# Transposing LayerNorm row tiles by a DMA transfer instead of by TensorE

## The chip, the core and the metric

The kernel runs on one NeuronCore of a Trainium2 chip. The metric is the device time of one execution in microseconds, from start to end as the runtime measures it. Lower is better.

## What is computed

Four residual layers over one sequence of 2048 rows and 576 features, in bf16: attention, gated MLP, attention, gated MLP. Each layer first normalises its input row by row (no learned scale). The attention is local and dilated: 32 heads of 18 features, and each position looks at itself and the seven positions 2, 4, ..., 14 rows before it. The gated MLP has a spatial product, in which a 2048x2048 matrix mixes the rows.

```python
def _layernorm(x, axis=-1, eps=1e-05):
    m = jnp.mean(x, axis=axis, keepdims=True)
    v = jnp.var(x, axis=axis, keepdims=True)
    return (x - m) / jnp.sqrt(v + eps)

def _A_ref(x, wqkv, wo):            # W, dil = 8, 2
    ...
    idx = pos[:, None] - off[None, :]
    ...
    logits = jnp.einsum('bhsd,bhswd->bhsw', q, kg) * scale
    attn = _softmax(jnp.where(mask, logits, -1000000000.0), axis=-1)
    o = jnp.einsum('bhsw,bhswd->bhsd', attn, vg)
    return o.transpose(0, 2, 1, 3).reshape(B, S, D) @ wo

def _B_ref(x, w_in, w_sp, b_sp, w_out):   # F = 4608, Fh = 2304
    z = _gelu(jnp.einsum('bsd,df->bsf', x, w_in))
    z1 = z[..., :Fh].copy()
    z2 = _layernorm(z[..., Fh:], axis=-1)
    g = jnp.einsum('ts,bsf->btf', w_sp, z2) + b_sp[None, :, None]
    return jnp.einsum('bsf,fd->bsd', z1 * g, w_out)

x = x + _A_ref(_layernorm(x, axis=-1), A_wqkv, A_wo)
x = x + _B_ref(_layernorm(x, axis=-1), B_w_in, B_w_sp, B_b_sp, B_w_out)
x = x + _A_ref(_layernorm(x, axis=-1), A_wqkv, A_wo)
x = x + _B_ref(_layernorm(x, axis=-1), B_w_in, B_w_sp, B_b_sp, B_w_out)
```

## The kernel before

The kernel has five phases: F (0 to about 252 us of the profiled execution), S (to 572), F (to 888), S (to 1206) and E (to the end).

**Phase F** makes an attention layer and the second half of the following MLP's input product. It is a pipeline of small steps, each on one engine. In order:

- *Row tiles for the attention.* There are 16 tiles of 128 rows. In the first F phase `LNX_steps` loads a tile of the input (x_in) and normalises it. In the second, `p3_steps` first makes the tile: it multiplies zu, the result of the S phase before, by the output weights (p_ps), adds the residual (x, L323), stores the sum to DRAM (xres) and normalises it.
- *`ln_steps`* is the normalisation, shared by all: `.s` takes statistics on VectorE (ln_st), `.p` makes the scale and offset on GpSimd, `.n` writes the normalised rows xn (bf16, 640 columns: 512 and the last 64 twice) on ScalarE, `.t` transposes xn by five TensorE transposes against the identity into PSUM (ln_tp), and `.e` copies that to xnD on VectorE or ScalarE, whichever the planner finds free.
- *xnD* is the transposed activation: 128 partitions, five chunks of features, and one column for each row of the sequence, with PADL = 14 columns of zeros ahead of row 0. All later products read it.
- *Queries and keys* (`QK_steps`): nine groups of 228 new columns, five products each (qk_ps), copied to stg, written to a DRAM buffer (qk_bounce) and read back in another layout (QK).
- *Values* (`V_steps`) and *attention* (`ATT_steps`): 18 tiles of 114 rows. L_ps is the logits, P the exponentials, O_ps the weighted values, o_t the quotient; w_ps is the output product, xw the new residual, stored to xres. Each such tile is then normalised by `ln_steps` too (114 rows, the last 110) and overwrites its columns of xnD.
- *`Z2_steps`* multiplies xnD by the second half of the input weights (z_ps), with GELU and normalisation into zu.

**Phase S** makes the first half of the input product from xnD and w1 (z_ps, L739), the spatial product (g_ps, L746, 32 matmuls for each of 72 tiles) and the gating. The spatial matrix w_sp comes transposed into W: four transfers of 512x2048 for each phase, issued from SP at L727. **Phase E** is the last output product.

The order of the work within a phase F is not written by hand. `Flow` takes the steps with their engine, an estimated duration, a key (smaller goes first), what they come after, and the buffers that they take (`caps`: three PSUM tiles H, two PT for transposes, three xn, three xw, three x in the second F phase). `order` plays them through and issues each engine's instructions in the order found. Each engine then works its queue in that order, and waits on hardware semaphores only. A step's successor may start `lag` after its end in the planner's time; 0.12 us for a compute step, and 2.2 to 6 us for a transfer (LX for a load, LW for a bounce write, LR for the read back). A buffer is free again, for the planner, at the end of its last user. The keys of the row tiles are `2 * g - KX` for the group g that needs them, those of QK group g `2 * g - KQ`, and those of attention tile t are about t; one key unit is one attention tile. All transfers within a phase F, save a few weights, go through SP's queue (`self.dma`, L164).

The matmuls of the values read xnD with a column step of 2. `wrote_xn` and `read_xn_strided` tell the framework which of these and which writes of xnD share columns.

Of the kernel before, what the change touches and what calls it, by code (L numbers as in the profile page):

```python
# [16 lines left out]
P = 128  # L17
HP = 64
S = 2048
# [7 lines left out]
QT = P - HALO  # L27
QH = QT // 2
PADL = HALO
NT = 18  # L30
NS = S // P
NG = NT // 2
GW = 2 * QT + HALO
GH = GW // 2
XW = QT * (NT - 1) + P
NB = 9
NZ = 10
NM = D // P
WA = 6
EPS = 1e-5  # L40
LX, LW, LR, KQ, KX = 5, 5.0, 6.0, 6.5, 8.0
SCALE = DH ** -0.5


# [104 lines left out]
class K:  # L149
# [16 lines left out]
    def setup(self):  # L166
        nc, tc, ctx = self.nc, self.tc, self.ctx
        c = self.base = ctx.enter_context(tc.tile_pool(name="base", bufs=1))
        self.dram = ctx.enter_context(tc.tile_pool(name="dram", bufs=1, space=DRAM))
        self.xres = [self.dram.tile([S, D], f32, name=f"xres{i}") for i in range(3)]  # L170
        self.ps = ctx.enter_context(tc.tile_pool(name="ps", bufs=1, space=PSUM))
        self.ident = c.tile([P, P], bf16, name="ident")
        self.maskT = c.tile([P, QH], bf16, name="maskT")
        self.mask0 = c.tile([P, QH], bf16, name="mask0")
        self.xnD = c.tile([P, NM + 1, XW], bf16, name="xnD")
        self.zu = c.tile([P, NZ, 2 * S], bf16, name="zu")
        self.wA = c.tile([P, WA * 2, D], bf16, name="wA")
        self.neg_half = c.tile([P, 1], f32, name="neg_half")
        make_identity(nc, self.ident[:])
        nc.vector.memset(self.neg_half[:], -0.5)  # L180
        self.xn_writes, self.xn_strided = [], []
        self.wrote_xn(nc.vector.memset(self.xnD[:, :, 0:PADL], 0.0), 0, PADL)
        self.wrote_xn(nc.vector.memset(self.xnD[:, :, PADL + S:XW], 0.0), PADL + S, XW)

    def masks(self):

# [56 lines left out]
        if not rest_first:  # L243
            rest(False)

    def ln_steps(self, fl, tag, key, row0, n, x, after, uses=(), guard=()):

        nc, pool, box = self.nc, self.pool, {}

        def stats(_):  # L250
            st = box["st"] = pool.tile([P, 2 * nc.vector.BN_STATS_DIM + 4], f32, name="ln_st", bufs=6)
            m = 2 * nc.vector.BN_STATS_DIM
            v = st[:, 0:m].rearrange("p (s d) -> p s d", s=2)
            box["s"] = [st[:, m + k:m + k + 1] for k in range(4)]
            for s in range(2):
                nc.vector.bn_stats(out=v[:n, s, :], in_=x()[:n, s * 288:(s + 1) * 288])  # L256
            nc.vector.bn_aggr(out=st[:n, m:m + 2], in_=v[:n, :, :])  # L257

        def small(_):
            mean, var, rstd, nmr = box["s"]  # L260
            nc.gpsimd.tensor_scalar_add(out=rstd[:n], in0=var[:n], scalar1=EPS)  # L261
            nc.gpsimd.tensor_tensor(out=rstd[:n], in0=rstd[:n], in1=self.neg_half[:n, :], op=ALU.pow)
            nc.gpsimd.tensor_scalar(out=nmr[:n], in0=mean[:n], scalar1=rstd[:n], scalar2=-1.0,
                                    op0=ALU.mult, op1=ALU.mult)

        def norm(_):
            xn = box["xn"] = pool.tile([P, D + HP], bf16, name="xn", bufs=3)
            mean, var, rstd, nmr = box["s"]
            last = x()[:n, None, NM * P:D].to_broadcast([n, 2, HP])
            for out, in_ in ((xn[:n, 0:NM * P], x()[:n, 0:NM * P]),  # L270
                             (xn[:n, NM * P:].rearrange("p (a b) -> p a b", a=2), last)):
                nc.scalar.activation(out=out, in_=in_, func=ACT.Identity, scale=rstd[:n], bias=nmr[:n])  # L272

        def trans(_):
            tp, xn = self.PTt("ln_tp"), box["xn"]
            box["tp"] = tp
            for c in range(NM + 1):
                nc.tensor.transpose(tp[:, c, :n], xn[:n, c * P:c * P + P], self.ident[:n, :n])  # L278

        cols = slice(PADL + row0, PADL + row0 + n)  # L280

        def evac(e):
            self.wrote_xn(self.copy(e, self.xnD[:, 0:5, cols], box["tp"][:, :, :n]), cols.start, cols.stop)

        fl.step(tag + ".s", "DVE", 1.15, key, stats, after, uses, takes=[("ln_st", tag + ".st")])
        fl.step(tag + ".p", "POOL", 1.2, key, small, [tag + ".s"], [tag + ".st"])
        fl.step(tag + ".n", "ACT", 1.15, key, norm, [tag + ".p"], [tag + ".st", *uses], takes=[("xn", tag + ".xn")])
        fl.step(tag + ".t", "PE", 0.3, key, trans, [tag + ".n"], [tag + ".xn"], takes=[("PT", tag + ".tp")], mode="w")
        fl.step(tag + ".e", ("DVE", "ACT"), 0.72, key, evac, [tag + ".t", *guard], [tag + ".tp"])

# [7 lines left out]
    def p3_steps(self, fl, i, key, wout, x_prev, li, after=()):  # L298
# [43 lines left out]
        if last:  # L342
            fl.step(tag + ".o", "ACT", 0.7, key, toout, [tag + ".a"], [tag + ".x"], takes=[("ob", tag + ".ob")])
            fl.step(tag + ".w", "SP", 0.35, key, store, [tag + ".o"], [tag + ".ob"], lag=2.2)
        else:
            fl.step(tag + ".w", "SP", 0.35, key, store, [tag + ".a"], [tag + ".x"], lag=2.2)
            self.ln_steps(fl, tag, key, i * P, P, lambda: box["x"], [tag + ".a"], [tag + ".x"])

# [1 line left out]
    def phase_F(self, li):  # L352
# [52 lines left out]
        def LNX_steps(i, key):  # L405
            box, tag = {}, f"lnx{i}"

            def load(_):
                box["x"] = pool.tile([P, D], bf16, name="x_in", tag="xb", bufs=8)
                self.dma(box["x"][:], self.A_x[i * P:(i + 1) * P, :])  # L410
            fl.step(tag + ".l", "SP", 0.4, key - 3 if i > 1 else -30, load, takes=[("xb", tag + ".x")], lag=2.2 if i < 2 else LX)
            self.ln_steps(fl, tag, key, i * P, P, lambda: box["x"], [tag + ".l"], [tag + ".x"])

        def feeds(c0, n):

# [5 lines left out]
        def QK_steps(g, key):  # L421
# [5 lines left out]
            for d in range(5):  # L427
                M = 126 if d < 4 else 72

                def mm(rest_first, d=d, M=M):  # L430
                    ps = box[d] = self.Ht("qk_ps")
                    cols, at = slice(126 * d, 126 * d + M), slice(c0, c0 + GW)
                    self.mm576(lambda s: ps[:M, s, 0:GW], rest_first,
                               lambda s, c: (wqk[:, c, s, cols], self.xnD[:, c, at]),
                               lambda s, rows: (wqk_r[rows, cols], self.xnD[rows, NM, at]))

                def ev(e, d=d, M=M):
                    stg = box[d, "s"] = pool.tile([P, 2, 2, GH], bf16, name="stg", bufs=6)
                    self.copy(e, stg[:M], box[d][:M, :, 0:GW].rearrange("p q (j r) -> p q r j", r=2))

                def wr(_, d=d, M=M):
                    self.dma(box["bn"][126 * d:126 * d + M], box[d, "s"][:M])
                fl.step(f"{tag}.m{d}", "PE", 1.02, key, mm, feeds(c0, GW) + ["wqk"], takes=[("H", f"{tag}.ps{d}")], mode="wn")
                fl.step(f"{tag}.e{d}", ("DVE", "ACT"), dict(DVE=0.67, ACT=0.58), key, ev, [f"{tag}.m{d}"], [f"{tag}.ps{d}"],
                        takes=[("stg", f"{tag}.s{d}")])
                fl.step(f"{tag}.w{d}", "SP", 0.4, key, wr, [f"{tag}.e{d}", tag + ".b"], [f"{tag}.s{d}", tag + ".bn"],
                        lag=LW)
# [11 lines left out]
        def V_steps(t, key):  # L459
            box, v = {}, vb[t % 3]  # L460

            def mm(rest_first):
                ps = box["ps"] = self.Ht("v_ps")
                c0 = QT * t

                def part(first, wide):
                    for c in range(NM) if wide else (NM,):
# [130 lines left out]
        def Z2_steps(i, key, after):  # L598
# [5 lines left out]
            def mm(u):  # L604
                def f(rest_first):
                    ps = box[u] = self.Ht("z_ps")
                    at, cols = slice(PADL + i * P, PADL + i * P + P), slice(384 * u, 384 * u + 384)
                    self.mm576(lambda s: ps[:, s, 0:384], rest_first,
                               lambda s, c: (self.xnD[:, c, at], (win2a[:, c, s] if c < NM - 1 else win2b[:, s])[:, cols]),
                               lambda s, rows: (self.xnD[rows, NM, at], win2r[rows, cols]))  # L610
                return f
# [94 lines left out]
    def phase_S(self, li):  # L706
# [21 lines left out]
        for jj in range(NB):  # L728
# [6 lines left out]
            z2 = self.zu[:, jj, :].rearrange("p (i s r) -> p i s r", i=NS, s=2)  # L735
            for q in range(4):
                ps = self.Ht("z1_ps")
                at = slice(PADL + 512 * q, PADL + 512 * q + 512)
                self.mm576(lambda s: ps[:, s, :], q % 2 == 1, lambda s, c: (w1[:, NM * s + c, :], self.xnD[:, c, at]),  # L739
                           lambda s, rows: (w1[rows, 2 * NM, :], self.xnD[rows, NM, at]))  # L740
                nc.scalar.activation(out=u[:, :, 512 * q:512 * (q + 1)], in_=ps[:], func=ACT.Gelu_apprx_tanh)  # L741
# [87 lines left out]
```

## Time and profile before

| | |
|---|---|
| median of 3 runs | 1278.86 us (1276.73 to 1284.46) |
| the profiled execution's own time | 1280.8 us |
| its span, first to last instruction | 1278.8 us |
| mean granted TensorE clock | 0.989 |
| busy: TensorE, VectorE, ScalarE, GpSimd | 1239.6, 556.4, 414.1, 198.6 us |
| first F phase / second F phase | 0 to 252 us / 572 to 888 us |
| transposes of normalised tiles (L278) | 340, five for each of 68 tiles |

The page gives each engine's busy time and its share of the span. In its table of slices the span is cut into 40 equal parts, and each digit is a busy share in tenths. Windows of time give busy microseconds and, in brackets, the number of instructions of each engine, then the granted TensorE clock as a share of full speed, and the DMA engines' mean busy share and rate. PEld is TensorE's weight load, which overlaps its matmuls. SPq is SP's instruction queue, from which transfers are issued.

### The profile page before, as it was taken

To read this page: it belongs to the slowest core of one execution; us is meant where nothing else is said; L and a number is where in the kernel's file an instruction comes from. 1 tells how busy PE (TensorE), PEld (TensorE's weight loads), DVE (VectorE), ACT (ScalarE), POOL (GpSimd) and SP (SyncE) were. 2 spreads that over 40 slices of the span, in tenths; PEclk is the share of its full clock that TensorE was granted. 3 is DMA by queue.
4 is the path that set the end of the run, shared out by engine and by line. 5 is a ranking of instruction groups with operands and counts; after the bars stand their busy time and mean duration, and the time that the engine had idled before them with its cause. 6 is when DMAs were issued, how large, how long until landed. Compare 5 with 4: busy or idle time off the path is not lost.

```text
span 1278.8 us, 27787 instructions
## 1 busy us (share of the span) xinstructions
PE 1239.6 (97%) x12182; PEld 728.2 (57%) x12244; DVE 556.4 (44%) x901; ACT 414.1 (32%) x662; POOL 198.6 (16%) x494
## 2 busy tenths in 40 slices
PE   7999989999999999999999999999999999999998
PEld 6787755444444444448788876554444444444576
DVE  5777666523232323334455675663333232222311
ACT  5744687701111111001435456875100011111011
POOL 5211146700000000001112111575000000000000
PEclk9999899999999999999999998999999999999999
DMA  7655315560000000035545354185300000000232
GB/s 201 165 147 143 87 34 101 122 156 10 10 10 10 10 10 1 1 104 172 148 129 142 110 136 136 34 169 112 99 2 10 10 10 10 10 1 1 79 104 68
DMA packets 142877, 96.31 MB, mean 75 GB/s; under 512 B 92084, under 2 KB 127604, under 8 KB 142756
## 3 DMA queue, kind: packets, MB, share of 16 engines
q1 hardware_dynamic: 142068, 92.17, 28.1%
q0 software_dynamic: 688, 2.38, 0.7%
q8 instruction: 95, 1.56, 0.5%
q14 instruction: 26, 0.21, 0.1%
HBM read 51.19 MB, written 26.55 MB: 61 GB/s over the span
## 4 chain that ended last, share of the span: by engine, by line
PE 89%; DVE 4%; ACT 2%; POOL 2%; issue 1%; DMA 1%; SPq 0%; POOLq 0%; DVEq 0%; ACTq 0%
PE g_ps L746 39%; PE z_ps L241 19%; PE p_ps L316 11%; PE qk_ps L241 6%; PE z_ps L235 3%; PE O_ps L523 3%; PE v_ps L471 3%; PE w_ps L570 2%; PE ln_tp L278 1%; PE qk_ps L235 1%; ACT xn L272 1%; PE o_tp L550 1%; DVE ln_st L256 1%; DVE xw L575 1%; DMA wB<-in_B_w_in_dram 1%
## 5 line engine op out<-in xcount | busy, mean ns | idle before, releaser
L746 PE MATMUL g_ps<-W,zu 128*128 128x512 bf16 x2256 | 497.7, 379 | 2.5
L746 PEld LDWEIGHTS <-zu 128*128 128x128 bf16 x2304 | 225.4, 98 | 271.8
L751 DVE TENSOR_TENSOR g_tmp<-g_ps,bsp 128x512 f32<-128x512 f32 x144 | 99.0, 687 | 437.9 <-PE g_ps L746 437.9
L741 ACT ACTIVATE zu<-z_ps 128x1024 bf16<-128x1024 f32 x72 | 73.7, 1023 | 514.4 <-PE z_ps L235 477.1
L241 PE MATMUL z_ps<-xnD,w 128*128 128x512 bf16 x562 | 132.1, 379 | 1.2 <-issue 0.6
L316 PEld LDWEIGHTS <-zu 128*128 128x128 bf16 x1152 | 111.7, 98 | 31.2 <-DVE zu L752 2.1
L241 PE MATMUL z_ps<-wA,xnD 128*128 128x384 bf16 x576 | 109.9, 327 | 3.9 <-DVE xw L575 3.9
L316 PE MATMUL p_ps<-wA,zu 128*128 128x288 bf16 x768 | 106.0, 286 | 0.5 <-ACT v_ext L296 0.5
L241 PEld LDWEIGHTS <-xnD 128*128 128x128 bf16 x768 | 70.8, 98 | 59.8 <-issue 18.5
L752 DVE TENSOR_TENSOR zu<-g_tmp,zu 128x512 bf16<-128x512 f32 x144 | 99.7, 692 | 9.6
L241 PEld LDWEIGHTS <-w 128*128 128x128 bf16 x576 | 52.7, 97 | 75.2 <-issue 15.7
L241 PE MATMUL qk_ps<-xnD,wqk 128*126 128x242 bf16 (+1 forms) x720 | 91.3, 275 | 2.9 <-DVE o_t L532 1.3
L615 ACT ACTIVATE zu<-z_ps 128x768 bf16<-128x768 f32 x96 | 77.1, 804 | 34.5 <-PE z_ps L235 20.6
L241 PEld LDWEIGHTS <-wqk 128*126 128x126 bf16 (+1 forms) x720 | 76.6, 135 | 10.5 <-issue 7.0
L508 ACT ACTIVATE P<-L_ps 128x912 bf16<-128x912 f32 x72 | 65.0, 943 | 18.1 <-PE L_ps L501 18.0
L625 DVE CUSTOM_DVE_ANT_1 zu<-zu 128x1536 bf16<-128x1536 bf16 x32 | 56.3, 1758 | 29.9 <-ACT zu L615 29.9
L261 POOL TENSOR_SCALAR ln_st<-ln_st 114x1 f32<-114x1 f32 (+1 forms) x68 | 20.1, 296 | 306.7 <-DVE ln_st L257 245.5
L323 DVE TENSOR_TENSOR x<-p_ps,x 128x576 f32<-128x576 f32 x32 | 24.2, 758 | 89.3 <-PE p_ps L316 89.3
L295 DVE CAST stg<-qk_ps 126x484 bf16<-126x484 f32 (+1 forms) x64 | 42.2, 660 | 32.0 <-PE qk_ps L235 20.1
L570 PE MATMUL w_ps<-wo,oT 128*114 128x288 bf16 (+1 forms) x360 | 52.4, 292 | 1.6 <-ACT zu L615 1.4
L471 PE MATMUL v_ps<-wv,xnD 128*64 128x288 bf16 x576 | 46.4, 310 | 1.9 <-DVE o_t L532 1.2
L523 PE MATMUL O_ps<-v_ext,P 64*64 64x19 bf16 x2304 | 43.6, 176 | 4.5 <-issue 1.6
(79 smaller groups left out, 1114.3 us busy)
## 6 DMA issues: line engine op xcount, KB each, us to landing
QK<-qk_bounce SPq DMA_DIRECT2D x72, 136.1 KB
x<-xres SPq DMA_DIRECT2D x32, 288.0 KB
xres<-xw SPq DMA_DIRECT2D x34, 256.5 KB
qk_bounce<-stg SPq DMA_DIRECT2D x72, 119.1 KB
w<-in_B_w_in_dram SPq DMA_DIRECT2D x36, 128.0 KB
xres<-x SPq DMA_DIRECT2D x16, 288.0 KB
xw<-xres SPq DMA_DIRECT2D x17, 256.5 KB
wA<-in_B_w_in_dram SPq DMA_DIRECT2D x12, 288.0 KB
```

The lines of the kernel that those rows point to most:

```text
L241: nc.tensor.matmul(ps(s), lhsT=lhsT, rhs=rhs, start=(c == 0 and not rest_first), stop=(c == NM - 1 and rest_first))
L316: nc.tensor.matmul(ps[:, hh, 0:288], lhsT=u[:, s * S + i * P:s * S + (i + 1) * P], rhs=wout(b, s)[:, hh * 288:(hh + 1) * 288], start=(b == ...
L471: self.read_xn_strided(nc.tensor.matmul(ps[HP * par:HP * par + HP, s, 0:288], lhsT=self.xnD[rows, c, c0 + par:c0 + P:2], rhs=wv[:, c, s, : ...
L508: nc.scalar.activation(out=Psb[:, 2 * hh:2 * hh + 2, :, 0:QH], in_=box["L"][hh][:, :, 0:8 * QH].rearrange("p a (b c) -> p a b c", c=QH), f ...
L523: nc.tensor.matmul(O[rows, h // 16, (h % 16) * (DH + 1):(h % 16 + 1) * (DH + 1)], lhsT=Psb[rows, h % 4, h // 4, :], rhs=v[rows, h, :], sta ...
L570: nc.tensor.matmul(box["ps"][:n, hh, 0:288], lhsT=box["oT"][:, c, :n], rhs=wo[:, c, hh * 288:(hh + 1) * 288], start=(c == 0), stop=(c == 4))
L615: nc.scalar.activation(out=self.zu[:, 3 * u:3 * u + 3, 256 * i:256 * (i + 1)].rearrange("p j (s r) -> p s j r", s=2), in_=box[u][:, :, 0:3 ...
L625: nc.vector.tensor_tensor_reduce(out=junk(0, 6), in0=z[:, 0:6, :], in1=z[:, 0:6, :], scale=1.0 / FH, scalar=0.0, op0=ALU.mult, op1=ALU.add ...
L741: nc.scalar.activation(out=u[:, :, 512 * q:512 * (q + 1)], in_=ps[:], func=ACT.Gelu_apprx_tanh)
L746: nc.tensor.matmul(ps[:, s, :], lhsT=z2[:, i, s, :], rhs=W[q][:, i, :], start=(i == 0), stop=(i == NS - 1))
L751: nc.vector.tensor_tensor(out=tmp[:], in0=ps[:, s, :], in1=bsp[:, 512 * q:512 * (q + 1)], op=ALU.add)
L752: nc.vector.tensor_tensor(out=uv, in0=tmp[:], in1=uv, op=ALU.mult)
```

## The change

Three things change.

1. For tiles of 128 rows, `ln_steps` has a second path (`by_dma`). The steps `.t` (TensorE) and the copy are gone; `.e` becomes one transposing transfer from xn (SBUF) to xnD (SBUF), issued from SP, planned at 1.3 us and a lag of LT = 5.0. In the first F phase tiles 4 to 15 take it, in the second all 16. The 36 tiles of 114 or 110 rows keep the old path.
2. xnD's columns move by OFF = 2, so that row 0 stands at column 16, and the row pitch becomes 2080 columns (4160 bytes). A tile's columns then begin on a multiple of 32 bytes. All readers move with it, and the two memsets of the borders are a little larger.
3. KX goes from 8.0 to 9.0: the row tiles' keys are one unit smaller. LX and LW keep their values.

```diff
-XW = QT * (NT - 1) + P
+OFF = 2
+XW = 2080
...
-LX, LW, LR, KQ, KX = 5, 5.0, 6.0, 6.5, 8.0
+LX, LT, LW, LR, KQ, KX = 5.0, 5.0, 5.0, 6.0, 6.5, 9.0
...
-    def ln_steps(self, fl, tag, key, row0, n, x, after, uses=(), guard=()):
+    def ln_steps(self, fl, tag, key, row0, n, x, after, uses=(), guard=(), by_dma=False):
...
-        cols = slice(PADL + row0, PADL + row0 + n)
+        cols = slice(OFF + PADL + row0, OFF + PADL + row0 + n)
+
+        def flip(_):
+            self.wrote_xn(nc.sync.dma_start_transpose(out=self.xnD[:, :, cols], in_=box["xn"][:]), cols.start, cols.stop)
...
         fl.step(tag + ".n", "ACT", 1.15, key, norm, [tag + ".p"], [tag + ".st", *uses], takes=[("xn", tag + ".xn")])
+        if by_dma:
+            fl.step(tag + ".e", "SP", 1.3, key, flip, [tag + ".n", *guard], [tag + ".xn"], lag=LT)
+            return
         fl.step(tag + ".t", "PE", 0.3, key, trans, [tag + ".n"], [tag + ".xn"], takes=[("PT", tag + ".tp")], mode="w")
...
-            self.ln_steps(fl, tag, key, i * P, P, lambda: box["x"], [tag + ".a"], [tag + ".x"])
+            self.ln_steps(fl, tag, key, i * P, P, lambda: box["x"], [tag + ".a"], [tag + ".x"], by_dma=True)
...
-            self.ln_steps(fl, tag, key, i * P, P, lambda: box["x"], [tag + ".l"], [tag + ".x"])
+            self.ln_steps(fl, tag, key, i * P, P, lambda: box["x"], [tag + ".l"], [tag + ".x"], by_dma=i > 3)
```

The remaining lines of the diff put OFF ahead of every column at which xnD is read or cleared.

More of the change, by code (lines that the diff above doesn't have):

```diff
@@ L181, in setup @@
         self.xn_writes, self.xn_strided = [], []
-        self.wrote_xn(nc.vector.memset(self.xnD[:, :, 0:PADL], 0.0), 0, PADL)
-        self.wrote_xn(nc.vector.memset(self.xnD[:, :, PADL + S:XW], 0.0), PADL + S, XW)
+        self.wrote_xn(nc.vector.memset(self.xnD[:, :, 0:OFF + PADL], 0.0), 0, OFF + PADL)
+        self.wrote_xn(nc.vector.memset(self.xnD[:, :, OFF + PADL + S:XW], 0.0), OFF + PADL + S, XW)
     def masks(self):
@@ L431, in mm @@
                     ps = box[d] = self.Ht("qk_ps")
-                    cols, at = slice(126 * d, 126 * d + M), slice(c0, c0 + GW)
+                    cols, at = slice(126 * d, 126 * d + M), slice(OFF + c0, OFF + c0 + GW)
                     self.mm576(lambda s: ps[:M, s, 0:GW], rest_first,
@@ L463, in mm @@
                 ps = box["ps"] = self.Ht("v_ps")
-                c0 = QT * t
+                c0 = OFF + QT * t
                 def part(first, wide):
@@ L606, in f @@
                     ps = box[u] = self.Ht("z_ps")
-                    at, cols = slice(PADL + i * P, PADL + i * P + P), slice(384 * u, 384 * u + 384)
+                    at, cols = slice(OFF + PADL + i * P, OFF + PADL + i * P + P), slice(384 * u, 384 * u + 384)
                     self.mm576(lambda s: ps[:, s, 0:384], rest_first,
@@ L737, in phase_S @@
                 ps = self.Ht("z1_ps")
-                at = slice(PADL + 512 * q, PADL + 512 * q + 512)
+                at = slice(OFF + PADL + 512 * q, OFF + PADL + 512 * q + 512)
                 self.mm576(lambda s: ps[:, s, :], q % 2 == 1, lambda s, c: (w1[:, NM * s + c, :], self.xnD[:, c, at]),
```

## The prediction

> **What bounds the kernel now.** I read the page's top first, then stages by windows of time, then the tile that the change concerns, then its nearest relatives on the DMA side. The page's engine line and slices:
>
> ```profile
> span 1278.8 us, 27787 instructions
> ...
> PE 1239.6 (97%) x12182; PEld 728.2 (57%) x12244; DVE 556.4 (44%) x901; ACT 414.1 (32%) x662; POOL 198.6 (16%) x494
> ...
> PE   7999989999999999999999999999999999999998
> ```
>
> TensorE is busy all through; the change touches only the two F phases (0 to 252 us, 572 to 888 us). The stages of these in which 128-row tiles are made (columns: window, its length, busy us and instructions of each engine, granted clock, DMA share, GB/s):
>
> ```profile
> core 0: us, PE busy (x) PEld busy (x) DVE busy (x) ACT busy (x) POOL busy (x), PEclk, DMA share, GB/s
> 14.00:60.00 46.00, 43.54 (x853) 36.42 (x851) 33.76 (x74) 31.14 (x54) 20.78 (x61) 1.00 0.71 178
> 60.00:100.00 40.00, 38.03 (x903) 31.98 (x899) 29.62 (x51) 20.13 (x31) 4.22 (x12) 0.96 0.57 150
> 100.00:150.00 50.00, 45.88 (x1186) 37.81 (x1181) 34.59 (x60) 26.07 (x39) 9.49 (x20) 0.92 0.49 125
> 572.00:640.00 68.00, 66.37 (x722) 53.14 (x721) 32.54 (x59) 19.25 (x29) 8.42 (x24) 1.00 0.61 167
> 640.00:720.00 80.00, 79.59 (x1494) 66.28 (x1492) 46.98 (x89) 36.86 (x56) 14.69 (x36) 1.00 0.45 128
> 720.00:782.00 62.00, 57.59 (x1438) 47.46 (x1437) 41.99 (x73) 36.00 (x53) 12.92 (x27) 0.93 0.51 135
> ```
>
> From 640 to 720 TensorE has 0.4 us to spare in 80, so a microsecond taken off it there is a microsecond of the kernel. In the first F phase it idles 2.5, 2.0 and 4.1 us in the three windows: part of a saving there only lengthens a wait.
>
> **What is removed.** The normalised tiles pass through ln_tp (columns: smallest, median, largest ns):
>
> ```profile
> L278 PE MATMUL ln_tp<-ident,xn x340: 209/219/314, 6.4 to 840.7; 114*128 114x114 bf16 x86, 128*128 128x128 bf16 x80, 110*128 110x110 bf16 x4
> L295 DVE COPY xnD<-ln_tp x36: 435/455/492, 7.1 to 841.0; 128x640 bf16<-128x640 bf16 x19, 128x570 bf16<-128x570 bf16 x15, 128x550 bf16<-128x550 bf16 x2
> L296 ACT COPY xnD<-ln_tp x32: 607/634/692, 16.7 to 784.1; 128x570 bf16<-128x570 bf16 x19, 128x640 bf16<-128x640 bf16 x13
> ```
>
> 68 tiles; the 36 of 114 or 110 rows keep their path, and so do the first four of 128 rows (i > 3). The transfer takes over 12 tiles in the first F phase and 16 in the second, 28 in all. Matmuls overlap, so 219 ns times five is not what a tile costs TensorE; that is the distance from its first transpose to the next instruction:
>
> ```profile
> 694.10 0.45 PE L278 MATMUL ln_tp<-ident,xn 128*128 128x128 bf16 x5
> 694.44 1.43 PE L570 MATMUL w_ps<-wo,oT 128*114 128x288 bf16 x10
> ```
>
> 0.34 us here; 0.28 at 618.28 (next instruction at 618.56) and 0.33 a tile at 30.47 (ten transposes, next at 31.13). I take 0.31: 28 x 0.31 = **8.7 us of TensorE**, 3.7 in the first F phase and 5.0 in the second. The evictions go too: of the 128x640 ones 16 on VectorE by about 0.46 and 12 on ScalarE by about 0.69, 7.4 + 8.3 = 15.7 us. Neither engine is over 75% busy in any window above, so I count nothing for these directly.
>
> **What it brings in my sum.** The second phase is nearly full: 0.95 x 5.0 = 4.7 us. In the first, a tile's slot is followed by waits of the attention chain, so I take half: 1.9 us. Together 6.6 us.
>
> **What is added: 28 transposing transfers on SP's queue.** No trace of before has one from SBUF to SBUF; the nearest is the transfer of W, 512x2048 each, from DRAM:
>
> ```profile
> L727 SPq DMA_TRANSPOSE W<-in_B_w_sp_dram x8: 7902/9070/10137, 211.5 to 885.5; - x8
> ```
>
> and its traffic, by windows of 1 us with TensorE alone (the last two columns are DMA share and GB/s):
>
> ```profile
> 212.00:213.00 1.00, 1.00 (x8) 1.00 0.04 10
> 213.00:214.00 1.00, 1.00 (x9) 1.00 0.90 184
> ...
> 239.00:240.00 1.00, 1.00 (x8) 1.00 0.48 105
> ```
>
> One holds SP 9.07 us for 64 blocks of 128x128, 0.14 us a block, and a tile has five: 0.7 us. The first W issue is at 211.48 and traffic begins just before 213, 1.4 us later; the third issue ends at 237.89 and traffic at about 239.5 (nothing from 240 on), 1.6 us later. So a tile should land about 0.7 + 1.4 + 0.7 + 1.5 = 4.3 us after its norm, an estimate that adds all four parts though they may overlap; today it is 1.1 us at the least (norm ended at 672.66, eviction at 673.78). From below it is bounded by start and traffic alone, 2.1 us; from above by the worst ordinary transfer on the chain of waits:
>
> ```profile
> 23.64 7.39 DMA qk_bounce<-stg
> ```
>
> 7.4 us, plus 0.7 of issue. I take 4.3, nearer the W row, since that is the same operation. The planner allows 1.3 + 5.0 = 6.3 us, and KX 9 instead of 8 asks for each tile one attention step earlier, so consumers are placed for 6.3. What hides 4.3 us is other TensorE work: in the second phase the p_ps matmuls (4.4 us a tile). Without it, each pair of tiles costs up to 3 us.
>
> The Trainium skill, VectorE: DVE Perf Modes (section The three transpose paths), speaks against the change: it gives 1309 ns for a 128x128 block by the DMA crossbar and 390 by TensorE, and advises TensorE where PSUM will do. By that figure five blocks in a row take an estimated 6.5 us, and the tile would land at about 10 us. The W row's 0.14 us a block disagrees, but it is a rate inside a large transfer; no run yet shows a small one.
>
> Where a price shows: tile 5 of the first phase. Its norm ends at 20.4 and group 2's qk_ps, its first reader, starts at 24.97. Landing at 24.7 it is in time, at the upper bound 3.5 us late; and the planner, which counts 6.3, places that reader at 26.7, 1.7 later, unless earlier norms or v_ps work fill the place. I take half, **0.9 us**. In the second phase tile 1's norm ends at 587.3, it lands at 591.6, and the first qk_ps is at 592.08: nothing.
>
> **SP.** From 640 to 700 it issues 44 transfers of about 0.34 us, a quarter of its time; a tile adds 0.7 us about every 9 us. A transposing transfer waits for ACT's norm, and behind it stand qk_bounce writes, QK reads, xres stores and loads; who waits for them is L_ps by way of QK, and the adds at L575 and L323. SP's waits on xn today (x loads that need a buffer) are at most 1.7 us. QK's path is planned with 5 + 6 us of slack, so I count nothing; uncovered, 28 x 0.9 (their mean today) would be 25 us of SP delay, little of it on TensorE. POOL's queue is not touched. The three xn buffers are held until the transfer has read them, some 3 us more; norms come four in 7 us at the densest (19.25 to 26.3, of 1.2 us each), so the fourth finds the first one's buffer free: nothing. xnD's shift costs nothing: weight loads from xnD and from zu take 98 ns alike, 512-column matmuls on either 379. The larger memsets (0.16 us now) lie before the first input lands.
>
> **Sum.** 1280.8 (profiled execution; span 1278.8 and 2.0 around it) - 6.6 + 0.9 = 1275.1. That execution is 1.9 above the median of the runs, so beside 1278.9 the forecast is **1273**, bounds of this case 1268 (all 8.7 us, and 2 more from the freed engines) to 1277.
>
> **Rivals.**
>
> *Waits shrink as well (1263).* Gaps trigger slow stretches of the clock:
>
> ```profile
> 80.00:84.00 4.00, 2.72 (x137) 1.00 0.58 130
> 84.00:88.00 4.00, 4.00 (x30) 0.57 0.74 168
> ```
>
> 1.3 us idle, then 4 us at 0.57, 1.7 us lost. Summed over all such windows, (1 - clock) x 4 is 6.8 us in each F phase. The idle times hang on VectorE and ScalarE (o_t, v_ext, P), which lose 15.7 us of work. If half of the 13.6 goes with the full 8.7: 1278.9 - 8.7 - 6.8 = 1263. Against it: most gaps lie after 80 us and after 740, where the last 128-row tiles are already done.
>
> *The slots become waits (1279).* Tiles land in time for the plan, but the new order puts idle time where the transposes were. For it: 8.6 us are idle already between 14 and 150. Against it: 640 to 720.
>
> *Late tiles, slower (1294).* The transfer queues in order behind the bounce and weight traffic (DMA share 0.71 from 14 to 60, 0.61 from 572 to 640), and lands later than the 6.3 us for which its readers were placed. TensorE is in order, so qk_ps holds up all behind it, and each gap of 1.3 us buys a slow stretch: 3.0 us. From seven of 18 groups on: 7 x 3.0 - 6 = +15. The 7.39 us on the chain speaks for it, W's 290 GB/s and the planned 6.3 against. By the Trainium skill's figure above every group would be late.
>
> **How the numbers follow.** The forecast 0.36; waits shrink too 0.25; slots become waits 0.12; late tiles 0.27. A measurement of this kernel can tell about 1% (1266 to 1292): faster is the second case, slower the fourth, the other two lie within. The range, 1262 to 1298, leaves out about a tenth at each end: the lower half of the second case, and of the fourth what has more than eight late groups. The likeliest case's own range is 1268 to 1277.
>
> **What would show it.** Right: 28 DMA_TRANSPOSE on xnD of about 0.7 us on SP; L278 x200; 640 to 720 still full, and F phases shorter by some 2 and 4.5 us; no TensorE wait on xnD's transfer above 1 us save near 25 us in the first phase; S phases unchanged. Wrong: waits of qk_ps or v_ps on a transfer of xnD, more stretches with the clock near 0.57, or an SP hold of several us a tile.

## The result, and the profile after

The changed kernel is slower: 1296.63 us median of 6 runs (1290.82 to 1304.13) against 1277.98 (1275.12 to 1284.46), a ratio of 1.0138 with a 95% interval of 1.0095 to 1.0181. The forecast was 1273. The profiled execution is the slowest of the six (1304.13 us, span 1302.4), so its losses are somewhat larger than the median's.

The head of the page of the changed kernel:

```profile
span 1302.4 us, 27608 instructions
...
PE 1244.8 (96%) x12104; PEld 729.9 (56%) x12104; DVE 551.5 (42%) x888; ACT 406.1 (31%) x647; POOL 197.8 (15%) x494
...
PE   7778889999999999999999998999999999999998
...
PEclk9779989999999999999999998999999999999999
```

The first six slices, 0 to 195 us, now hold 7s and 8s, and the clock row shows two 7s near the start. The rest is as before. The same in windows (columns as in the prediction), the first three in the first F phase, the others in the second, which starts 24.4 us later than before:

```profile
14.00:60.00 46.00, 37.28 (x609) 30.30 (x610) 25.19 (x56) 24.91 (x41) 19.69 (x57) 0.83 0.87 173
60.00:100.00 40.00, 33.09 (x621) 27.10 (x616) 19.71 (x35) 16.56 (x27) 5.21 (x13) 0.81 0.64 133
100.00:150.00 50.00, 44.73 (x1051) 37.67 (x1051) 35.09 (x59) 22.72 (x33) 7.18 (x15) 0.97 0.53 135
...
597.00:665.00 68.00, 66.36 (x695) 53.37 (x694) 32.04 (x60) 16.17 (x25) 9.47 (x27) 1.00 0.89 189
665.00:745.00 80.00, 75.85 (x1389) 63.92 (x1385) 45.83 (x85) 33.67 (x51) 12.64 (x36) 0.96 0.57 139
745.00:807.00 62.00, 56.29 (x1489) 46.79 (x1484) 41.77 (x73) 32.91 (x49) 10.91 (x24) 0.97 0.54 140
```

From 14 to 100 us TensorE idles 15.6 us where it idled 4.4 before, and works at a mean clock of 0.83 and 0.81 where it had 1.00 and 0.96. The first S phase's first z_ps comes at 274.9 us against 250.5: the profile's whole 24 us are lost in the first F phase. The second takes 306.3 us from its first p_ps to its last z_ps of wB, against 306.7: neither loss nor gain in these two executions. An estimate from the windows above and those of before: from 14 to 150 us TensorE idles 20.9 us against 8.6, and the slow clock, counted as in the prediction as (1 - clock) times the length of a window, is worth 16.9 us against 5.6. About half of the 24 us is idle time, and about half the slow clock that comes with it.

The tile's own instructions and the transfer:

```profile
L279 PE MATMUL ln_tp<-ident,xn x200: 209/213/314, 6.4 to 864.8; 114*128 114x114 bf16 x86, 128*128 128x128 bf16 x10, 110*128 110x110 bf16 x4
...
L284 SPq DMA_TRANSPOSE xnD<-xn x28: 1204/1217/2629, 19.8 to 757.5; - x28
```

140 transposes are gone and 28 transfers are there, each holding SP for 1.2 us at least. Who waits for what on ScalarE in the first 150 us (total us, times, longest):

```profile
ACT stg L303 <- DMA qk_bounce<-stg: 20.1, 5, 5.4
...
ACT xn L273 <- DMA xnD<-xn: 11.9, 3, 6.0
```

and before:

```profile
ACT stg L296 <- DMA qk_bounce<-stg: 4.3, 1, 4.3
```

The second did not exist before. The copies of qk_ps wait for a stg buffer whose bounce write has not landed, and the norm waits for an xn buffer that a transposing transfer has not read. ScalarE works in order, so all behind them is late. Four transfers stand on the chain between 14 and 110 us (start, us, what):

```profile
23.42 2.68 DMA xnD<-xn
...
30.25 7.52 DMA xo<-in_A_x_dram
...
37.84 8.22 DMA qk_bounce<-stg
...
61.82 6.82 DMA xnD<-xn
```

A load, a bounce write and the second transposed tile take 6.8 to 8.2 us; the planner counted 5 for each (6.3 with the issue for the tile). The first tile took 2.68. What differs is the company. The three stretches in which ScalarE's norm waited for the buffer of a tile, from the tile's issue to the end of the wait (with three buffers it is the tile three before; the last two columns are DMA share and GB/s; a share above 1 is packet times that overlap):

```profile
23.42:26.09 2.67, 2.67 (x40) 1.86 (x40) 1.20 (x4) 2.06 (x5) 2.14 (x9) 1.00 0.69 153
27.66:34.39 6.73, 6.52 (x122) 5.25 (x118) 3.19 (x5) 0.64 (x1) 2.92 (x7) 1.00 1.11 176
61.82:68.64 6.82, 3.19 (x32) 2.52 (x30) 3.08 (x6) 0.94 (x2) 1.05 (x3) 0.99 1.18 152
```

At a share of 0.69 the buffer is held 2.7 us, at 1.11 and 1.18 it is held 6.7 and 6.8. And the gap that follows buys a slow clock (the windows with TensorE alone: busy us, clock, DMA share, GB/s):

```profile
40.00:44.00 4.00, 1.40 (x12) 1.00 0.81 159
44.00:48.00 4.00, 1.10 (x42) 0.58 0.84 155
48.00:52.00 4.00, 3.13 (x102) 0.50 0.78 201
52.00:56.00 4.00, 3.81 (x81) 0.50 0.65 158
56.00:60.00 4.00, 4.00 (x82) 0.50 1.11 146
```

5.5 us of idle time from 40 to 48, then twelve microseconds at half the clock.

### The profile page after: what moved, and what is told of

Same layout as the page of the kernel before. It is cut to its first block, busy times and chain, and to the rows that moved or that the text cites. A ratio compares the mean times of both kernels' runs of the same rounds, so it can differ in the third digit from the quotient of the medians.

```text
span 1302.4 us, 27608 instructions
## 1 busy us (share of the span) xinstructions
PE 1244.8 (96%) x12104; PEld 729.9 (56%) x12104; DVE 551.5 (42%) x888; ACT 406.1 (31%) x647; POOL 197.8 (15%) x494
## 3 DMA queue, kind: packets, MB, share of 16 engines
q1 hardware_dynamic: 160884, 96.76, 31.7%
## 4 chain that ended last, share of the span: by engine, by line
PE 88%; DVE 5%; DMA 3%; issue 2%; ACT 1%; POOL 1%; SPq 0%; DVEq 0%; ACTq 0%; POOLq 0%
PE g_ps L753 38%; PE z_ps L242 19%; PE p_ps L323 10%; PE qk_ps L242 6%; PE v_ps L478 4%; PE w_ps L577 3%; PE z_ps L236 3%; PE O_ps L530 2%; DMA xnD<-xn 1%; PE qk_ps L236 1%; DMA qk_bounce<-stg 1%; PE o_tp L557 1%; DVE o_t L539 1%; DVE xw L582 1%; PE ln_tp L279 1%
## 5 line engine op out<-in xcount | busy, mean ns | idle before, releaser
L242 PE MATMUL qk_ps<-xnD,wqk 128*126 128x242 bf16 (+1 forms) x720 | 97.5, 286 | 10.7 <-DVE o_t L539 6.0
L242 PEld LDWEIGHTS <-w 128*128 128x128 bf16 x576 | 53.2, 98 | 74.6 <-issue 15.6
L242 PEld LDWEIGHTS <-wqk 128*126 128x126 bf16 (+1 forms) x720 | 80.5, 141 | 20.4 <-issue 11.2
L262 POOL TENSOR_SCALAR ln_st<-ln_st 128x1 f32<-128x1 f32 (+1 forms) x68 | 18.4, 270 | 332.4 <-DVE ln_st L258 293.1
L577 PE MATMUL w_ps<-wo,oT 128*114 128x288 bf16 (+1 forms) x360 | 57.8, 311 | 1.6 <-ACT zu L622 1.4
L273 ACT ACTIVATE xn<-xw,ln_st 114x512 bf16<-114x512 f32 (+1 forms) x72 | 43.0, 646 | 40.4 <-POOL ln_st L264 34.4
```

What stands on the lines that cost most here:

```text
L242: nc.tensor.matmul(ps(s), lhsT=lhsT, rhs=rhs, start=(c == 0 and not rest_first), stop=(c == NM - 1 and rest_first))
L577: nc.tensor.matmul(box["ps"][:n, hh, 0:288], lhsT=box["oT"][:, c, :n], rhs=wo[:, c, hh * 288:(hh + 1) * 288], start=(c == 0), stop=(c == 4))
```

## The experiments

### Which phase, and is it the order or the shift

**f2_only**: the change in the second F phase alone.

```diff
-            self.ln_steps(..., [tag + ".l"], [tag + ".x"], by_dma=i > 3)
+            self.ln_steps(..., [tag + ".l"], [tag + ".x"])
```

> The change as it is in the second F phase (16 tiles), the old path in the first. In the profiles the first phase ends 24.4 us later with the change (first z_ps of the S phase at 274.9 against 250.5) and the second takes as long as before (306.6 against 306.9 us). Theory A (crowded transfers in the first phase): the loss is all in the first phase, so 1274 to 1280 us, level with before. Theory B (the new order of the work, which is made in both phases): part of the loss stays, 1283 to 1290. Theory C (shift of the columns): the loss stays, about 1295.

Measured: 1277.59 us, ratio 0.9975 (0.9952 to 0.9997). (A ratio is to the kernel before, measured beside it; in brackets its 95% interval.) The loss lies in the first F phase; theory A as far as the place goes.

**late_plan**: all tiles by TensorE, in an order that counts on late tiles.

```diff
-        if by_dma:
-            fl.step(tag + ".e", "SP", 1.3, key, flip, ..., lag=LT)
-            return
...
-        fl.step(tag + ".e", ("DVE", "ACT"), 0.72, key, evac, ...)
+        fl.step(tag + ".e", ("DVE", "ACT"), 0.72, key, evac, ..., lag=LT if by_dma else None)
```

> Transposes by TensorE and the copy as before, but the planner is told that the 28 tiles land 5 us after their copy, and KX is 9: the order of a kernel that counts on late tiles, without a transfer. Theory A (crowded transfers): no transfer, no loss, 1274 to 1283 us. Theory B (the order): most of the loss, 1290 to 1298.

Measured: 1274.73 us, ratio 0.9969 (0.9949 to 0.9990). Planned lateness alone costs nothing. Theory B falls as far as it says that any order that counts on late tiles is slow. The change's own order is not this one, though: the planner counts 1.3 us of SP for each transfer and keeps the xn buffer until then, and in the traces SP's issues part at 19.3 us, where late_plan loads xo. The change's own order without transfers was not run.

**off_only**: path, KX and order of before, xnD's columns of after (the edit against the kernel before).

```diff
-XW = QT * (NT - 1) + P
+OFF = 2
+XW = 2080
...
```

> Only xnD's shift to a 32-byte boundary and the larger pitch; path, KX and order as before. Theories A, B and D: level with before, 1275 to 1283 us. Theory C (the shift costs): 1290 or more.

Measured: 1279.82 us, ratio 0.9994 (0.9973 to 1.0015). The shift costs nothing. Theory C falls. The order is before's in both phases, so its trace also shows how far one execution can be from another. Before's window from 640 to 720 us, in which TensorE idled 0.4 us, is here:

```profile
640.00:720.00 80.00, 76.98 (x1388) 63.77 (x1386) 44.55 (x83) 34.47 (x52) 13.63 (x33) 0.96 0.44 123
```

3.0 us of idle time, and a clock of 0.96.

### Load without dependence

**ring_load**: before's path and KX, and 12 transposing transfers into scratch, from xn buffers of their own.

```diff
+            scr = self.zu[:, j // 6, 640 * (j % 6):640 * (j % 6) + 640]
+            nc.sync.dma_start_transpose(out=scr.rearrange("p (c r) -> p c r", r=P), in_=box["xn"][:])
...
+            fl.step(tag + ".d", "SP", 1.3, key, flip, [tag + ".n"], [tag + ".xn"], lag=LT)
```

> The old path for all tiles, KX 8; beside it, 12 of the first phase's tiles (4 to 15) are also transposed by a transfer from SP into scratch that nobody reads, from buffers of their own that are never taken again while a transfer reads them. So SP's 1.2 us each and the DMA engines' load are there, and nobody waits for the tile or for its xn buffer. Theory A (crowded transfers: the bounce and load transfers on the same rings land late, and engines wait for stg buffers and QK): most of the loss, 1288 to 1300 us. Theory D (only what waits for the transposed tiles and their xn buffers is late): 1277 to 1283.

Measured: 1284.35 us, ratio 1.0040 (1.0020 to 1.0060). Between the two theories: about 6 us (1.0040 against 0.9994 of off_only, the same path without the load), not the whole loss. The planner counts the scratch transfers too, so the order is neither before's (SP's issues part at 18.7 us) nor the change's. The same with the change's planned lateness and KX:

**late_load**: late_plan with the 12 scratch transfers, again from xn buffers of their own.

> The order of the change without its dependence: all tiles go by TensorE and the copy, the planner is told that the 28 tiles land late and KX is 9 (which alone measured 0.997 of before), and 12 tiles of the first F phase are also transposed by a transfer into scratch from buffers of their own. If the engines' load in this order makes bounce and load transfers late, that is the loss: 1288 to 1296 us. If the load is tolerable in any order (1.004 in the old order) and only the wait for transposed tiles costs: 1275 to 1283.

Measured: 1289.85 us, ratio 1.0078 (1.0055 to 1.0101). Beside late_plan that is 1.0078 - 0.9969 = 1.09%, some 14 us (about 4 either way, from the two intervals), for transfers whose result nobody reads. The expectation calls this the order of the change; it is not, and it is not late_plan's either. SP's issues part from late_plan's at 19.3 us and TensorE's steps at 52.5, so the 14 us are the transfers and the order planned around them together. The next experiment takes them apart. In late_plan ScalarE and in late_load ScalarE wait for stg so, from 14 to 150 us:

```profile
ACT stg L301 <- DMA qk_bounce<-stg: 0.3, 1, 0.3
```

```profile
ACT stg L309 <- DMA qk_bounce<-stg: 9.7, 2, 5.6
```

The bounce writes come later beside transfers that have nothing to do with them.

### What in the transfer costs

**alone**: the transfers by themselves in the first S phase, at times when nothing else moves.

```diff
+            nc.gpsimd.tensor_copy(out=src[:, 0:512], in_=tmp[:])
...
+                nc.sync.dma_start_transpose(out=d, in_=src[:])
...
+                nc.sync.dma_start(out=dst[:, k, :], in_=src[:])
...
+            nc.gpsimd.tensor_copy(out=got[:, k, :], in_=dst[:, k, 128 * n - 1:128 * n])
```

> The kernel before, with transfers by themselves added in the first S phase, where the DMA engines are idle between weight loads: a transposing transfer of a 128x640 tile from SBUF to SBUF, a plain copy of the same tile, a transposing transfer of one 128x128 block, another whole tile, and two tiles one behind the other. Each is issued from SP when GpSimd has filled the source, and GpSimd reads the last column as soon as it has landed. The recorded prediction's step: 0.7 us of traffic and at most 4.3 us from issue to landing. From the change's trace (DMA time up by 53.5 us of 16 engines over 28 tiles): about 1.9 us of traffic, so two in a row land 2 us apart, and the plain copy is much quicker, under 1 us of traffic.

Measured, one execution. SP's queue and GpSimd's reader of the landed tile, for a whole tile and for a plain copy of it:

```profile
342.03 1.22 SPq L733 DMA_TRANSPOSE dst<-src  x1
...
377.98 0.51 SPq L735 DMA_DIRECT2D dst<-src  x1
```

```profile
344.66 0.19 POOL L742 COPY got<-dst 128x1 bf16<-128x1 bf16 x1 [2.66 <-DMA dst<-src]
...
380.20 0.19 POOL L742 COPY got<-dst 128x1 bf16<-128x1 bf16 x1 [2.25 <-DMA dst<-src]
```

and the tile's traffic, by 0.2 us (clock, DMA share, GB/s):

```profile
343.20:343.40 0.20, 1.00 0.77 160
343.40:343.60 0.20, 1.00 1.09 216
343.60:343.80 0.20, 1.00 1.09 215
343.80:344.00 0.20, 1.00 1.00 197
344.00:344.20 0.20, 1.00 0.18 31
```

Alone, a tile lands 2.63 us after its issue starts, the plain copy after 2.22, a single block after 2.37. Traffic starts 1.2 us after the issue and lasts 0.85 us, 0.86 us of all 16 engines (share 0.33 over 2.6 us); the second of two tiles in a row lands 1.3 us after the first. My 1.9 us of traffic for a tile was wrong for a tile alone. The recorded 4.3 us was cautious, as it was meant to be. So nothing in the transfer by itself makes the loss. What is left is its meeting with others, and the order.

**load_block** and **load_copy**: late_load with one block for five, and with plain copies for the transposing transfers.

```diff
-            nc.sync.dma_start_transpose(out=scr.rearrange("p (c r) -> p c r", r=P), in_=box["xn"][:])
+            nc.sync.dma_start_transpose(out=scr.rearrange("p (c r) -> p c r", r=P)[:, 0:1, :], in_=box["xn"][:, 0:P])
```

> As late_load (1.008 of before, 1.1% over the same order without transfers), but each of the 12 scratch transfers transposes one 128x128 block instead of five. By itself such a transfer holds SP 1.15 us against 1.22 and moves a fifth of the bytes. If the loss comes from the traffic: 0.996 to 1.000 of before, 1274 to 1279 us. If it comes from SP's 1.2 us a tile, with bounce and load transfers queued behind: it stays, 1.005 to 1.010, 1285 to 1292 us.

Measured: 1282.34 us, ratio 1.0017 (0.9993 to 1.0040), between the two cases.

```diff
-            nc.sync.dma_start_transpose(out=scr.rearrange("p (c r) -> p c r", r=P), in_=box["xn"][:])
+            nc.sync.dma_start(out=scr, in_=box["xn"][:])
```

> As late_load, but the 12 scratch transfers are plain copies of the same 160 KB; alone one holds SP 0.51 us and moves at 280 to 380 GB/s where the transposing one moves at 200 to 220. If bytes on the rings are what costs: 1.004 to 1.008, 1284 to 1290 us. If it is the transposing transfer's own slowness (in the first F phase it takes 2.3 to 2.8 us of all engines, 0.86 alone): 0.997 to 1.002, 1275 to 1282.

Measured: 1284.07 us, ratio 1.0027 (1.0000 to 1.0054), by its ratio between the two cases, its interval reaching into both. The queue's lines of load_copy and of late_load (packets, MB, share of 16 engines):

```profile
q1 hardware_dynamic: 143796, 94.14, 28.1%
```

```profile
q1 hardware_dynamic: 150132, 94.14, 29.6%
```

Against late_plan's 142068 packets a copied tile is 144 packets and a transposed one 672, of the same bytes. Over the spans (1272.5, 1289.5 and 1282.2 us; late_plan's share is 27.9%) a copied tile takes 0.6 us of all engines and a transposed one 2.0. late_load, load_block and load_copy share one order: SP's other issues and TensorE's steps come in the same sequence in the three traces. So what they differ by is the transfers alone. Five transposed blocks cost 0.61% more than one, some 8 us, and 0.51% more than plain copies of the same bytes, some 6.5 us; each of these is uncertain by about 4 us, and neither interval of the two reaches late_load's. What load_block has over late_plan, 0.48% or some 6 us, is SP's holds, a fifth of the traffic and the other order, which these runs do not divide. load_block and load_copy cannot be told apart. ScalarE's waits for stg in the same order, in load_block and in load_copy:

```profile
ACT stg L309 <- DMA qk_bounce<-stg: 3.1, 1, 3.1
```

```profile
ACT stg L309 <- DMA qk_bounce<-stg: 8.7, 2, 4.6
```

With late_load's 9.7 they follow the bytes, copied or transposed, and not the time. These are one execution each (load_copy's is its slowest, late_load's its fastest), so by which wait the transposing costs more than the copying is not shown.

### What waits

**xn_free**: the change, with an xn buffer for every row tile of the first F phase, in zu, and the same order.

```diff
+            if tag[:3] == "lnx":
+                j = int(tag[3:])
+                xn = box["xn"] = self.zu[:, 6 + j // 6, 640 * (j % 6):640 * (j % 6) + 640]
```

> The change with its order untouched; in the first F phase each of the 16 row tiles has an xn buffer of its own (in zu, which is idle then), so ScalarE's norm never waits until a transfer has read an older xn. In the profile of the change ScalarE waited so three times, 11.9 us in all, all in the first phase. Theory D1 (this hold is the loss): 1277 to 1283 us. Theory A1 (the late bounce transfers hold the stg buffers, 27.5 us of waits of ScalarE and VectorE): little comes back, 1290 to 1297. Both alike: 1284 to 1289.

Measured: 1289.69 us, ratio 1.0064 (1.0036 to 1.0092), between "both alike" and "little comes back". The order is the change's own, so the difference, 1.0138 - 1.0064 = 0.74% or some 9 us (about 6.5 either way), is the held xn buffer. ScalarE's waits on it are gone from the trace. In their place TensorE waits for a tile, and a piece of the chain from a tile's issue to its landing lasts 9.4 us:

```profile
PE qk_ps L242 <- DMA xnD<-zu: 4.0, 1, 4.0
```

```profile
29.04 9.44 DMA xnD<-zu
```

**stg16**: 16 stg buffers in the first F phase instead of 6.

```diff
+                    if first:
+                        k = (5 * g + d) % 16
+                        stg = self.zu[:, 4 + k // 8, 484 * (k % 8):484 * (k % 8) + 484]
```

> The change with its order untouched; in the first F phase the copies of qk_ps go to 16 stg buffers in turn instead of 6, so ScalarE and VectorE do not wait for a bounce write that lands late. Theory A1 (stg is the loss): 1277 to 1285 us. Theory D1 (xn is): 1290 to 1297. If neither buffer matters and late QK reads and tiles do, both kernels stay at 1290 or above.

Measured: 1296.38 us, ratio 1.0138 (1.0098 to 1.0177): nothing comes back, in four runs. The stg waits, the longest line in ScalarE's list, were not the loss. With more buffers they are gone, and ScalarE waits 14.4 us in four times for the xn buffer, where it was 11.9 in three; on the chain a bounce write of 6.5 us and the QK read behind it, 7.3, follow each other.

**both_free**: both.

> Both of these together. If the two holds are the whole loss of the first phase: 1272 to 1281 us, at or under before. If the lateness of tiles and of QK itself weighs beside them: 1284 or more.

Measured: 1293.05 us, ratio 1.0105 (1.0052 to 1.0158), in four runs; the interval overlaps xn_free's. The two holds are not the whole loss. Beside stg16 the free xn buffers bring 0.33% here, less than xn_free's 0.74%, but the intervals hold both. In its chain a QK read of 8.26 us and an x_in load of 6.78 us follow each other.

**act_ring**: the transposing transfers issued from ScalarE.

```diff
-            self.wrote_xn(nc.sync.dma_start_transpose(...
+            self.wrote_xn(nc.scalar.dma_start_transpose(...
...
-            fl.step(tag + ".e", "SP", 1.3, key, flip, ...
+            fl.step(tag + ".e", "ACT", 1.3, key, flip, ...
```

> The change with the transposing transfers issued from ScalarE's queue, right behind the norm, in both phases; SP keeps the rest. The planner takes 1.3 us of ScalarE for each. Theory that SP's in-order queue (a transfer that waits for its norm or for the engines, with bounce and load transfers behind it) makes them late: 1275 to 1283 us. Theory that the 16 engines are short of time (about 1.9 us of all of them for a tile): the loss stays, 1290 to 1300, and 28 x 1.2 us of ScalarE come on top.

Measured: 1289.98 us, ratio 1.0107 (1.0046 to 1.0169). Its interval, 1286 to 1302 us, lies above the first case (1275 to 1283) and holds the second and the change's own ratio: a queue of its own does not mend it. Whether it helps a little is open, in four runs and with the issue time now on ScalarE. On that queue a tile takes 2.2 us of all engines (4.7% of 1286.1 us over 28).

### The plan

**plan_real**: the change, the planner told the landings that the trace shows in the first F phase.

```diff
+        LX, LT, LW, LR = (7.0, 6.5, 8.0, 8.0) if first else (5.0, 5.0, 5.0, 6.0)
```

> The change with the planner told longer landings in the first F phase, as the traces show them: 7 us for loads, 6.5 after the issue of a transposed tile, 8 for a bounce write and 8 for the read back, instead of 5, 5, 5 and 6. If the loss is that the order counts on landings which are not kept: 1276 to 1286 us. If the engines have no time for it in any order, 1290 or more.

Measured: 1287.26 us, ratio 1.0073 (1.0049 to 1.0097), between the two cases.

**kx8**: the change with KX = 8.0.

> The change with KX back at 8. If asking for the tiles one attention tile earlier crowds the start (more loads and transposed tiles in the first 60 us): 1280 to 1288 us. If KX is not the cause: 1291 to 1299; if the earlier tiles help against late landings, above 1299.

Measured: 1289.62 us, ratio 1.0082 (1.0055 to 1.0109), between the first two cases.

**real_free**: xn_free and plan_real together.

> The change with both mendings that helped: an xn buffer for each tile in the first F phase (1.006) and the planner told longer landings (1.007). If they remove two different parts of the loss: 0.999 to 1.003, 1278 to 1284 us. If both remove the same part and the load is the rest: 1.005 to 1.008, 1285 to 1290.

Measured: 1288.59 us, ratio 1.0060 (1.0039 to 1.0081). Three different mendings (a buffer for each tile, honest landings, tiles asked for later) each end at 1.006 to 1.008, and two of them together no lower, which is the second case. late_load is at 1.008, too; that what cannot be mended so is the load is an argument from these equal figures, not shown.

### A version that beats both

**best**: the change in the second F phase, TensorE's transposes in late_plan's order in the first.

```diff
-        if by_dma:
+        if by_dma and tag[0] == "p":
...
-        fl.step(tag + ".e", ("DVE", "ACT"), 0.72, key, evac, ...)
+        fl.step(tag + ".e", ("DVE", "ACT"), 0.72, key, evac, ..., lag=LT if by_dma else None)
```

> The change in the second F phase; in the first, TensorE's transposes in the order of late_plan (a planned lag of 5 us for tiles 4 to 15, KX 9). If the two small gains measured (0.9975 for the second phase alone, 0.9969 for the order) add: 0.994 to 0.996, 1271 to 1275 us. If they are one gain (KX 9 is in both): 0.997, 1275 to 1277.

Measured: 1276.54 us, ratio 0.9955 (0.9940 to 0.9970), faster than before by 0.45% and than the change by 1.8%. It differs from the change in how 12 tiles are transposed and in the order that the planner makes for that; its first F phase has late_plan's order. The 12 transfers and their order cost 1.0138 - 0.9955 = 1.83%, 23 us. late_load over late_plan is 14 us and xn_free's part 9; that they add up so well is partly luck, with some 4 to 6.5 us of uncertainty on each.

## Why the prediction was wrong

- **The sign.** The likeliest case, 1268 to 1277 us, failed; 1296.63 lies in the whole range only by the rival of late tiles (chance 0.27, 1294 us). That rival had the late transfers and the slow clock right. Its sum did not happen as written: it had TensorE's qk_ps held up by the tile in seven groups, and TensorE waited for tiles 1.3 us in all. That its time is so near is partly luck.
- **SP's hold, 0.7 us.** It is 1.22. The W row's 9.07 us over 64 blocks was used as a price per block; one block alone holds SP 1.15 us, so for a tile nearly all of it is the same for one block as for five. In the change it is up to 2.6.
- **Traffic, 0.7 us, and landing, 4.3.** Alone the traffic is 0.85 us and the landing 2.6, under the estimate. Among the bounce writes and loads of the first F phase a tile adds 2.0 to 2.8 us of all engines (2.0 in late_load; 2.8 in the change: 31.7% of 1302.4 us less f2_only's 29.8% of 1274.3, over 12), and its buffer was still held 6.7 and 6.8 us after the issue where the DMA engines were busy throughout. The step added parts of a transfer measured outside the crowded stretch. The upper bound, 7.4 + 0.7, was the nearer row, and xn_free's 9.4 us is over it; the DMA share of 0.71 from 14 to 60 us was the sign.
- **"QK's path ... I count nothing."** This is the largest term that was left out. It priced SP's delay, not what the transfer does to those that share the DMA engines. In one order, with no reader of the tile, five transposed blocks cost 8 us more than one and 6.5 more than copies; late_load as a whole is 14 over late_plan, with the order's part in it.
- **"The fourth finds the first one's buffer free: nothing."** The hold was put at 3 us. In the three cases in which the norm waited it was 2.7, 6.7 and 6.8 after the issue, which in the last two came 3.8 and 5.0 us behind the norm, and the waits 0.3, 5.7 and 6.0 us: 9 us of the kernel by xn_free, about 6.5 either way.
- **The second phase, 4.7 us.** The profiles show 0.4 (the change), and best against late_plan 0.14%, some 1.8 us, with intervals that overlap. The slots did go. But from 665 to 745 TensorE idles 4.2 us where it idled 0.4 in the window that I called full, and that 0.4 was one execution's. off_only, with before's path and order, idles 3.0 us there, and late_plan, also without transfers, 2.9 us in the like window. The whole phase, from its first p_ps to its last z_ps of wB, takes 306.7, 308.5 and 303.6 us in before, off_only and ring_load, which have one order there: single traces scatter by as much as the 4.7 that I forecast. How much of the saving became waits, and whether a gain of a few us is hidden in the second phase, is open.
- **The sign to look for.** I named qk_ps waiting on a transfer of xnD. In the change TensorE waited for that 1.3 us in all; the longer waits for transfers are those of ScalarE and VectorE. With the xn buffers freed the sign does come, 4.0 us in one wait.
- **The Trainium skill, VectorE: DVE Perf Modes (The three transpose paths).** Its 1309 ns for a block by the DMA crossbar spoke against the change, and that was the right side, but not by the sum made of it: alone, five blocks land 0.26 us after one, so the figure is not a price to multiply. It is near what one instruction holds SP here, 1.15 to 1.22 us.
- **Right:** the shift costs nothing (off_only), the count of tiles, and the coupling of a gap with a slow clock.

What stays open is the rest of the 14 us, some 6, which may be SP's holds, the little traffic of load_block, or the planner's other order. A run that plans the scratch transfers and leaves them out would settle it, and there is none; nor is there one with the change's own order and no transfers.

## What to carry to other kernels

Price a transfer in the company that it will have: a tile that lands in 2.6 us alone held its buffer 6.7 and 6.8 us where the DMA share was above 1.1, and it makes its neighbours late. A planner's landing times hold only as long as nothing is added to the transfers, and a buffer read by a transfer is free when the transfer has read it, not when it is issued. Before taking work off the bound engine, put the new load beside the old path with nobody waiting for it, and keep the order of all other work. Here the planner made another order for the extra steps, so only runs that share the steps and differ in the transfer (late_load, load_block, load_copy) show what the load alone costs.

## What the runs showed of the hardware

A transposing transfer of 160 KB from SBUF to SBUF goes as 672 packets, a plain copy of it as 144. Alone the two differ little (0.85 us at about 200 GB/s, landing at 2.63 against 2.22 us). In the first F phase (92084 of the 142877 packets of the kernel before are under 512 bytes) the transposed tile adds 2.0 us of the engines' time and the copied one 0.6. Alone, SP is held 1.15 us for one block and 1.22 for five; in the change up to 2.6. The tile's buffer was held 2.7 us after the issue at a DMA share of 0.69, and 6.7 and 6.8 at 1.11 and 1.18. After 5.5 us of idle time within 8 us the granted clock was 0.50 for twelve microseconds.
